# Products with v moved between the score units of an attention and feed-forward kernel

## The chip, the core and the metric

The kernel runs on one core of a Trainium2 chip. The metric is the device time of one execution in microseconds (us), the median of several runs. The engines are TensorE (PE in the profile, its weight loads PEld), VectorE (DVE), ScalarE (ACT), GpSimd (POOL) and SyncE (SP), which here issues nearly all DMAs.

## The reference

Attention with a decay from forget gates, for 4 batches of 8 heads with 576 queries and keys of 64 numbers, and then two feed-forward layers on the 2304 tokens of width 512, with 2048 hidden units:

```
scores = scale * q @ k.T
cum = cumsum(log(clip(f, 1e-4, 1)))
decay = cum[:, None] - cum[None, :]
attn = softmax(where(causal, -1e9, scores + decay))
x = attn @ v                       # heads laid side by side
h = x @ w_in;  x = (h - tanh(h)) @ w_out
h = x @ w_in2; out = (h * sigmoid(h)) @ w_out2
```

## The kernel before

The attention works on 16 pairs of heads, one after the other in a software pipeline. A pair is cut into nine score tiles, which form four **score units**: u = 0 has the first and second 128 queries of both heads (four tiles, with 128 and 256 keys), u = 1 the third 128 queries of both heads (384 keys), u = 2 the fourth (512 keys), u = 3 the last 64 queries of both heads together (576 keys, one tile, `pt`). Scores are computed with numbers split in a high and a low part (`kqs`), plus a product with the decay rows (`de`).

Each tile then goes through the engines. VectorE adds the mask and finds the row's minimum of the negated scores (`least`, tile `p` or `pt`, L462). ScalarE takes the exponent and the row sum (`expo`, L470). VectorE gathers three tiles' sums and takes reciprocals (`guard` L477, `normalise` L481). GpSimd scales three tiles (L484), in groups of tiles 0 to 2, 3 to 5 and 6 to 8 of a pair. TensorE transposes the scaled tiles in 128x128 blocks into PSUM tiles `t` (`transposes`, L495; 25 blocks a pair), VectorE and ScalarE copy them to `ptf` (`evac`, L535), TensorE multiplies `ptf` with `vraw` (`values`, L546), and ScalarE copies the result to `x` (`collect`, L554). Queries and keys of the next pair are split meanwhile: a cast of the keys on GpSimd (L383), a cast of the queries on VectorE (`split(p, 1)`, L385), and four subtractions on GpSimd (L391).

The order of everything is written by hand. The main loop runs over tile numbers n, nine to a pair, and every step is put at a number with `later` or `at`; each engine works through its own queue in that order. For pair p, with n0 = 9p, `steps_` gives the numbers of the transposes of the four units and of the values: n0 + 13, 15, 17, 18 and 26. Scores of a pair stand at n0 - 1, n0, n0 + 4 and n0 + 6. So while one pair is scored, the pair before it is transposed, and the values belong to the pair two before. `ends_` holds other numbers for the last two pairs. Score tiles have two PSUM buffers, transposed tiles (and a small output tile) three. In `transposes`, the fifth block of unit 3 takes a quarter of a PSUM tile, and the rest of that tile (`spare`) is used by unit 0 of the next pair.

The weights of the feed-forward part come as 64 bit numbers and are decoded in 14 steps a chunk (`wstages`): `scale` and `split` on ScalarE, `shift`, `exponent` and `low` on VectorE, `rest` and `join` (a subtraction and an addition, L176 and L180) on the engine `eng`. Chunks 0 and 1 are decoded during the attention, step by step at numbers spread evenly. The last part of the attention already has the first matmuls of the feed-forward part between its steps. The feed-forward part behind it isn't touched.

Of the kernel before, what the change touches and what calls it, by code (L numbers as in the profile page):

```python
# [7 lines left out]
F32 = mybir.dt.float32  # L8
# [6 lines left out]
P = 128  # L15
# [17 lines left out]
NEARLY, MID, LATE = 2, 3, 6  # L33
# [6 lines left out]
def forgetting_attention_two_ffn(  # L40
# [12 lines left out]
    nc = tc.nc  # L53
# [9 lines left out]
    def rd(ap):  # L63
        return ap.bitcast(F32)
# [21 lines left out]
    def setup_ident(const):  # L86
        ident = const.tile([P, P], F32, name="ident")
        nc.gpsimd.memset(ident, 0.0)
        nc.gpsimd.affine_select(
            out=ident, in_=ident, pattern=[[-1, P]], compare_op=ALU.not_equal,  # L90
            fill=1.0, base=0, channel_multiplier=1,
        )
        return ident
# [49 lines left out]
    def wstages(k):  # L143

        l, c = chunks[k]
        slot = k % NSLOT
        tag = {m: f"{l}_{c}_{m}" for m in range(2)}
        a, b, w = {}, {}, {}
        eng = nc.gpsimd if k < NEARLY + MID else nc.vector

        def scale(m):
            high = rd(raws[k, m][:, :, 1])
            nc.scalar.activation(high, high, AF.Prelu, scale=2.0 ** -112, alpha=-(2.0 ** 32))

        def shift(m):
            a[m] = wtmp.tile([P, DM], U32, tag="wa", name=f"wa{tag[m]}")
            nc.vector.tensor_scalar(a[m], raws[k, m][:, :, 1], 3, None, ALU.logical_shift_left)

        def split(m):
            hi, lo = w[m] = [  # L160
                wpool[slot].tile([P, DM], F32R, tag=f"w{s}{slot}_{m}", name=f"w{s}{tag[m]}") for s in "hl"
            ]
            nc.scalar.copy(hi, rd(a[m]))

        def exponent(m):
            b[m] = wtmp.tile([P, DM], F32, tag="wb", name=f"wb{tag[m]}")
            nc.vector.tensor_scalar(b[m].bitcast(U32), a[m], 0xFF800000, None, ALU.bitwise_and)

        def low(m):
            nc.vector.scalar_tensor_tensor(  # L170
                b[m], raws.pop((k, m))[:, :, 0], 2.0 ** -52, b[m], ALU.mult, ALU.mult
            )

        def rest(m):
            hi, lo = w[m]
            eng.tensor_tensor(lo, rd(a[m]), rd(hi), ALU.subtract)  # L176

        def join(m):
            hi, lo = w[m]
            eng.tensor_tensor(lo, rd(lo), b[m], ALU.add)  # L180
            wtiles[l, c, m] = (hi, lo)

        return [(fn, m) for fn in (scale, shift, split, exponent, low, rest, join) for m in range(2)]

    NSTAGE = 14
    stages = {}

    def wdecode(k, left=0):


        if k not in stages:
            stages[k] = wstages(k)
        while len(stages[k]) > left:
            fn, m = stages[k].pop(0)
            fn(m)
            if not stages[k] and k > 1:
                wload(k + 2)
# [7 lines left out]
    for l in range(2):  # L205
        c0 = 0
# [120 lines left out]
    def attention():  # L327
        with ExitStack() as actx:
# [4 lines left out]
            def pool(stack, name, bufs=1, **kw):  # L333
                return stack.enter_context(tc.tile_pool(name=name, bufs=bufs, side="right", **kw))
# [7 lines left out]
            ps_t = pool(actx, "ps_t", 3, space=PSUM)  # L342
# [4 lines left out]
            NP = B * NPAIR  # L347
# [5 lines left out]
            pt4 = [sp.tile([P, 640], F32, name=f"pt4_{i}", bufs=1) for i in range(2)]  # L353

            out_t = ps_r.tile([P, 512], F32, name="out_t")
            out_0, spare = {}, {}

            ptfs = [ptp.tile([P, 2, NPT], F32, name=f"ptf{i}") for i in range(2)]

# [58 lines left out]
            units = (((0, 0), (1, 0), (0, 1), (1, 1)), ((0, 2), (1, 2)), ((0, 3), (1, 3)), ((2, 4),))  # L418
            order = [t for unit in units for t in unit]
            NTILE = len(order)  # L420
            tiles = [(p, h, i) for p in range(NP) for h, i in order]
            N = len(tiles)
            sps, ptile, rowsum, tps = {}, {}, {}, {}
# [62 lines left out]
            def transposes(p, u):  # L486

                ptf = ptfs[p % 2]
                rest = spare.pop("t", None) if u == 0 else spare.clear()
                tp = [ps_t.tile([P, 4, P], F32, tag="t", name=f"t{p}_{u}_{j}") for j in range(1 if rest else 2)]  # L490
                if rest:
                    tp.append(rest[:, 1:])

                def turn(j, k, pt, c):
                    nc.tensor.transpose(tp[j][:, k], pt[:, c * P:c * P + P], ident)  # L495

                def place(j, c0, nc_, i):
                    n = 2 * nc_
                    q = P * i + 448 * c0
                    dst = ptf[:, :, q:q + 448 * nc_] if nc_ > 1 else ptf[:, :, q:q + P]  # L500
                    src = tp[j][:, 0:n]
                    if nc_ > 1:
                        dst = dst.rearrange("p h (c w) -> p h c w", w=448)[:, :, :, 0:P]
                        src = src.rearrange("p (h c) w -> p h c w", h=2)
                    return src, dst

                if u == 3:
                    ptile.pop((p, 2, 4))
                    pt = pt4[p % 2]
                    spare["t"] = tp[1]  # L510
                    for c in range(5):
                        turn(c // 4, c % 4, pt, c)
                    dst = ptf[:, :, 512:512 + 4 * 448].rearrange("p h (c w) -> p c h w", w=448)[:, :, :, 0:64]
                    o = 448 * 4 + 512
                    tps[p, u] = [
                        (tp[0].rearrange("p c (h w) -> p c h w", h=2), dst),
                        (tp[1][:, 0].rearrange("p (h w) -> p h w", h=2), ptf[:, :, o:o + 64]),
                    ]
                    return
                pts = {t: ptile.pop((p,) + t)[0] for t in units[u]}  # L520
                i = u + 1
                if u == 0:
                    for h in range(2):
                        turn(1, h, pts[h, 0], 0)
                for j in range(2 if u else 1):
                    for h in range(2):
                        for k in range(min(2, i + 1 - 2 * j)):
                            turn(j, min(2, i + 1 - 2 * j) * h + k, pts[h, i], 2 * j + k)
                tps[p, u] = [place(j, 2 * j, min(2, i + 1 - 2 * j), i) for j in range(2 if u else 1)]
                if u == 0:  # L530
                    tps[p, u].append(place(1, 0, 1, 0))

            def evac(p, u):
                for j, (src, dst) in enumerate(tps.pop((p, u))):
                    (nc.vector.tensor_copy if j == (u > 0) else nc.scalar.copy)(dst, src)  # L535

            def values(p, part):

# [56 lines left out]
            ident = setup_ident(const)  # L595
# [4 lines left out]
            def later(n, fn, *a):  # L600
                due.setdefault(max(n, 0), []).append((fn, a))
# [6 lines left out]
            for p in range(1, NP):  # L608
                n0 = NTILE * (p - 1)
                if p > 1:  # L610
                    if p > 2:
                        later(n0 - 9, load_kq, p)
                    later(n0 - 1, place_dec, p)
                    later(n0 - 1, place_dec_last, p)
                    later(n0 + (NTILE if p > 2 else 2 - NTILE), load_v, p)
                for j, k in enumerate((0, 0, 1, 2, 3, 4)):
                    later(n0 + k, split, p, j)
                later(n0 + 5, place_last, p)

            steps_ = (13, 15, 17, 18, 26)  # L620
            ends_ = {NP - 2: (13, 15, 17, 18, 20), NP - 1: (11, 12, 13, 14, 16)}
            for p in range(NP):
                n0 = NTILE * p
                for u, k in enumerate((-1, 0, 4, 6)):
                    if p + u:
                        later(n0 + k, scores, p, u)
                k = ends_.get(p, steps_)
                for u in range(4):
                    later(n0 + k[u], transposes, p, u)
                    later(n0 + k[u] + 1, evac, p, u)  # L630
                later(n0 + k[4], values, p, [(0, 0), (64, 0), (64, 1), (64, 2), (64, 3), (64, 4)])
                later(n0 + k[4] + 1, collect, p, 0, 64)
                later(n0 + k[4] + 1, collect, p, 64, S)
# [16 lines left out]
            def at(n, *item):  # L650
                ahead.setdefault(n, []).append(item)
# [3 lines left out]
                            (138, 3, 0), (140, 3, 1)):  # L655
                at(n - N, wload, k, (m,))
            for k in range(2 * NSTAGE):
                at((40, 87)[k // NSTAGE] + 46 * (k % NSTAGE) // NSTAGE - N,
                   wdecode, k // NSTAGE, NSTAGE - 1 - k % NSTAGE)
            for k in range(NKT):  # L660
                at(2 * k - 11, xsplit, 0, [k])
            for i in range(3):
# [80 lines left out]
```

## Time and profile before

| | before |
|---|---|
| median of 3 runs | 983.91 us (983.66 to 984.03) |
| profiled execution | 984.0 us, span 982.1 us |
| TensorE busy | 964.6 us, 98% |
| VectorE busy | 555.8 us, 57% |
| ScalarE busy | 454.8 us, 46% |
| GpSimd busy | 183.6 us, 19%, all of it in the first 208 us |
| granted TensorE clock | 1.000 |

Shares are over the whole span, of which the attention takes about the first 190 us. What a change in that part is worth has to be read there: from the windows and from the timeline of one pair. A timeline row gives the start, the time from the first start to the last end of the instructions it merges, the engine, the line, output <- inputs, the form, the count, and in brackets idle time ahead with what ended it.

### The profile page before, as it was taken

To read this page: it belongs to the slowest core of one execution; us is meant where nothing else is said; L and a number is where in the kernel's file an instruction comes from. 1 tells how busy PE (TensorE), PEld (TensorE's weight loads), DVE (VectorE), ACT (ScalarE), POOL (GpSimd) and SP (SyncE) were. 2 spreads that over 40 slices of the span, in tenths; PEclk is the share of its full clock that TensorE was granted. 3 is DMA by queue.
4 is the path that set the end of the run, shared out by engine and by line. 5 is a ranking of instruction groups with operands and counts; after the bars stand their busy time and mean duration, and the time that the engine had idled before them with its cause. 6 is when DMAs were issued, how large, how long until landed. Compare 5 with 4: busy or idle time off the path is not lost.

```text
span 982.1 us, 13857 instructions
## 1 busy us (share of the span) xinstructions
PE 964.6 (98%) x5208; PEld 791.5 (81%) x5208; DVE 555.8 (57%) x1221; ACT 454.8 (46%) x979; POOL 183.6 (19%) x266
## 2 busy tenths in 40 slices
PE   8999999999999999999999999999999999999998
PEld 6766666778988889888889888888888888888887
DVE  7667676686865456664668653354444544633323
ACT  6777777744543424343434443343444433433222
POOL 8979989740000000000000000000000000000000
PEclk9999999999999999999999999999999999999999
DMA  4433222421211011100112110111111000001111
GB/s 154 147 120 136 87 92 83 149 100 43 86 44 43 1 43 65 65 21 23 43 43 87 43 43 1 44 43 43 43 43 43 36 24 29 1 1 43 44 43 65
DMA packets 21699, 56.67 MB, mean 58 GB/s; under 512 B 6848, under 2 KB 6848, under 8 KB 21600
## 3 DMA queue, kind: packets, MB, share of 16 engines
q1 hardware_dynamic: 21624, 55.77, 16.1%
q8 instruction: 41, 0.67, 0.3%
q14 instruction: 26, 0.21, 0.1%
q10 hardware_dynamic: 8, 0.02, 0.0%
HBM read 49.35 MB, written 5.31 MB: 56 GB/s over the span
## 4 chain that ended last, share of the span: by engine, by line
PE 94%; DVE 3%; POOL 1%; issue 1%; DMA 0%; ACT 0%; SPq 0%; POOLq 0%; DVEq 0%
PE a L314 40%; PE h L255 39%; PE s L449 4%; PE out_t L546 4%; PE t L495 3%; PE s L441 2%; DVE p L462 1%; PE out_t L574 1%; POOL wl L180 1%; POOL wl L176 0%; DVE ptf L535 0%; PE out L546 0%; DMA kqraw<-kq 0%; DVE kqs L385 0%; POOL gl L277 0%
## 5 line engine op out<-in xcount | busy, mean ns | idle before, releaser
L255 PE MATMUL h<-xh,wl 128*128 128x512 f32 (+1 forms) x640 | 235.7, 368 | 2.2 <-POOL wl L180 2.2
L255 PE MATMUL h<-xh,wh 128*128 128x512 f32 (+1 forms) x640 | 236.0, 369 | 0.0
L255 PE MATMUL h<-xl,wh 128*128 128x512 f32 (+1 forms) x640 | 235.6, 368 | 0.0
L277 DVE TENSOR_TENSOR gl<-g,gh 128x512 fp32r<-128x512 f32 (+1 forms) x158 | 101.4, 642 | 99.9 <-ACT gh L273 98.0
L255 PEld LDWEIGHTS h<-xh,wl 128*128 128x128 f32 x640 | 120.6, 188 | 23.1 <-POOL wl L180 3.0
L255 PEld LDWEIGHTS h<-xh,wh 128*128 128x128 f32 x640 | 120.7, 189 | 20.6
L255 PEld LDWEIGHTS h<-xl,wh 128*128 128x128 f32 x640 | 120.6, 188 | 20.4
L273 ACT CAST gh<-g 128x512 fp32r<-128x512 f32 (+1 forms) x160 | 92.6, 579 | 95.8 <-DVE g L270 93.3
L314 PE MATMUL a<-gl,wh 128*128 128x512 f32 (+1 forms) x320 | 117.8, 368 | 0.0
L314 PE MATMUL a<-gh,wh 128*128 128x512 f32 (+1 forms) x320 | 117.7, 368 | 0.0
L314 PE MATMUL a<-gh,wl 128*128 128x512 f32 (+1 forms) x320 | 117.7, 368 | 0.0
L314 PE MATMUL a<-wh,gh 128*128 128x512 f32 x288 | 112.2, 390 | 0.0
L314 PE MATMUL a<-wl,gh 128*128 128x512 f32 x288 | 112.2, 390 | 0.0
L314 PE MATMUL a<-wh,gl 128*128 128x512 f32 x288 | 112.0, 389 | 0.0
L272 ACT ACTIVATE g<-h 128x512 f32<-128x512 f32 (+1 forms) x80 | 44.3, 554 | 113.6 <-PE h L255 96.3
L243 DVE TENSOR_TENSOR xl<-y,xh 128x512 fp32r<-128x512 f32 (+1 forms) x60 | 37.4, 638 | 96.6 <-ACT xh L241 96.6
L462 DVE CUSTOM_DVE_ANT_0 p<-s,mask 128x128 f32<-128x128 f32 (+3 forms) x128 | 59.9, 478 | 43.8 <-PE s L449 37.0
L241 ACT CAST xh<-y 128x512 fp32r<-128x512 f32 (+1 forms) x60 | 34.2, 580 | 104.8 <-PE h L255 103.1
L470 ACT ACTIVATE p<-p,mn 128x128 f32<-128x128 f32 (+3 forms) x128 | 71.1, 558 | 8.5 <-DVE mn L462 6.0
L484 POOL TENSOR_SCALAR p<-p,sm 128x128 f32<-128x128 f32 (+3 forms) x128 | 67.7, 548 | 18.3 <-DVE sm L481 18.3
L243 DVE TENSOR_TENSOR xl<-x,xh 128x512 fp32r<-128x512 f32 (+1 forms) x56 | 34.2, 632 | 61.6 <-ACT xh L241 61.6
L314 PEld LDWEIGHTS a<-gl,wh 128*128 128x128 f32 x320 | 60.3, 189 | 10.1
(92 smaller groups left out, 1388.9 us busy)
## 6 DMA issues: line engine op xcount, KB each, us to landing
raw<-w_in SPq DMA_DIRECT2D x32, 512.0 KB
raw<-w_out SPq DMA_DIRECT2D x32, 512.0 KB
kqraw<-kq SPq DMA_DIRECT2D x16, 608.0 KB
vraw<-v SPq DMA_DIRECT2D x16, 320.0 KB
out<-ob SPq DMA_DIRECT2D x18, 256.0 KB
lq<-kqs SPq DMA_DIRECT2D x32, 32.0 KB
dec<-x SPq DMA_DIRECT2D x1, 576.0 KB
de<-dec SPq DMA_DIRECT2D x28, 17.0 KB
```

The lines of the kernel that those rows point to most:

```text
L241: nc.scalar.copy(hi[:, :n], src[:, k, t0:t0 + n])
L243: eng.tensor_tensor(lo[:, :n], src[:, k, t0:t0 + n], rd(hi[:, :n]), ALU.subtract)
L255: nc.tensor.matmul(hp[:, :n], w[:, k * P:k * P + P], m[:, :n], start=(k == 0 and r == 0), stop=(k == NKT - 1 and r == 2),)
L272: nc.scalar.activation(g[:, :n], hp[:, :n], AF.Silu)
L273: nc.scalar.copy(gh[:, :n], g[:, :n])
L277: eng.tensor_tensor(gl[:, :n], g[:, :n], rd(gh[:, :n]), ALU.subtract)
L314: nc.tensor.matmul(dst, w, m, start=(first and r == 0), stop=(last and r == 2))
L449: nc.tensor.matmul(s[:, h, c:c + n], a[half(h), q], b[half(h), 0:n], start=r == 0, stop=r == 3,)
L462: nc.vector.tensor_tensor_reduce(out=pt.rearrange("p (g c) -> p g c", g=2) if i == 4 else pt, in0=src, in1=m, op0=ALU.add, op1=ALU.min, sc ...
L470: nc.scalar.activation(pt, pt, AF.Exp, bias=mn, scale=-1.0, accum_out=sums[:, n // 3 % 5, n % 3, 0:1],)
L484: nc.gpsimd.tensor_scalar(pt, pt, sm[:, j:j + 1], 1.0, ALU.mult, ALU.mult)
L546: nc.tensor.matmul(dst, vraw[p][:, h, D * c:D * c + D], ptfs[p % 2][:, h, 448 * c + a:448 * c + q1], start=c == 0, stop=c == last,)
```

## The change

It does four things. The values of a pair move from n0 + 26 to n0 + 22, that is, from behind the last transposes to between the second and the third score unit of the pair two behind, after unit 0's transposes. The transposes of unit 3 move from n0 + 18 to n0 + 15, into the call for unit 1 (three blocks of 128, 384 columns), except for the last pair: its fifth block goes into the half empty second PSUM tile of unit 1, its other four into a third tile. The cast of the queries moves from n0 to n0 - 1 of the pair before (n0 of `split`). And chunks 0 and 1 are decoded at other numbers, three steps to a pair from n = 37 to 118 (before: 40 to 82 and 87 to 129), their `rest` and `join` on VectorE in place of GpSimd.

```diff
-        eng = nc.gpsimd if k < NEARLY + MID else nc.vector
+        eng = nc.gpsimd if NEARLY <= k < NEARLY + MID else nc.vector
...
-                rest = spare.pop("t", None) if u == 0 else spare.clear()
-                tp = [ps_t.tile([P, 4, P], F32, tag="t", name=f"t{p}_{u}_{j}") for j in range(1 if rest else 2)]
-                if rest:
-                    tp.append(rest[:, 1:])
...
+                both = u == 1 and p < NP - 1
...
+                if u == 0:
+                    square(1, 0, 2, tile(0), 0, "V")
+                    square(0, 0, 1, tile(1), 0, "A")
+                elif u < 3:
+                    square(u + 1, 0, 2, tile(0), 0, "A")
+                    t = tile(1)
+                    square(u + 1, 2, u, t, 0, "V")
+                    if both:
+                        last_fifth(t, 2, "V")
+                        last_four(tile(2), "A")
+                else:
+                    last_four(tile(0), "A")
+                    last_fifth(tile(1), 0, "V")
...
-                for j, k in enumerate((0, 0, 1, 2, 3, 4)):
+                for j, k in enumerate((0, -1, 1, 2, 3, 4)):
...
-            steps_ = (13, 15, 17, 18, 26)
-            ends_ = {NP - 2: (13, 15, 17, 18, 20), NP - 1: (11, 12, 13, 14, 16)}
+            steps_ = (13, 15, 17, None, 22)
+            ends_ = {NP - 2: (13, 15, 17, None, 20), NP - 1: (11, 12, 13, 14, 16)}
...
-                for u in range(4):
+                for u in range(4 if k[3] else 3):
...
-                at((40, 87)[k // NSTAGE] + 46 * (k % NSTAGE) // NSTAGE - N,
-                   wdecode, k // NSTAGE, NSTAGE - 1 - k % NSTAGE)
+                at(NTILE * (4 + k // 3) + (1, 3, 5)[k % 3] - N, wdecode, k // NSTAGE, NSTAGE - 1 - k % NSTAGE)
```

`square`, `last_four` and `last_fifth` transpose the blocks of a unit and note the copy for `evac`; "A" is ScalarE and "V" VectorE. Copies stay on the engines they had, in size and number.

TensorE, one pair in the middle of the attention. In the names, `s_0` to `s_3` are the score units, `t_u_j` the transposed tiles of unit u, `out_` and `out_t` the products with v. Before:

```order
L449 MATMUL s_1_636<-kqs_498 128x384 x6
L449 MATMUL s_1_636<-de_103 128x384 x2
L495 MATMUL t_3_0_646<-ident,pt_1_107 128x128 x4
L495 MATMUL t_3_1_647<-ident,pt_1_107 128x128
L495 MATMUL t_3_1_647<-ident,p_0_446 128x128 x2
L495 MATMUL t_0_0_689<-ident,p_0_446 128x128 x4
L449 MATMUL s_2_696<-kqs_498 128x512 x6
```

After, at the same place:

```order
L449 MATMUL s_1_648<-kqs_484 128x384 x6
L449 MATMUL s_1_648<-de_103 128x384 x2
L496 MATMUL t_0_0_688<-ident,p_0_454 128x128 x4
L496 MATMUL t_0_1_693<-ident,p_0_454 128x128 x2
L552 MATMUL out_1_696<-ptf_110,vraw_194 64x64 x2
L552 MATMUL out_t<-ptf_110,vraw_194 64x512 x2
L552 MATMUL out_t<-ptf_110,vraw_194 64x448 x2
L552 MATMUL out_t<-ptf_110,vraw_194 64x320 x2
L552 MATMUL out_t<-ptf_110,vraw_194 64x192 x2
L552 MATMUL out_t<-ptf_110,vraw_194 64x64 x2
L449 MATMUL s_2_709<-kqs_484 128x512 x6
```

The transposes of unit 3 are gone from behind the second score unit, and the products with v stand in front of the third.

VectorE, from the reciprocal behind unit 3's minimum to the second minimum of the next pair (L385 is the cast of the queries). Before:

```order
L481 RECIPROCAL sm_624<-sm_624 128x3
L535 COPY ptf_110<-t_2_1_583 128x2x2x128
L462 ISA p_0_606,mn_0_0_658<-s_0_605,mask 128x128
L462 ISA mn_0_0_658 128x1
L385 TENSOR_REDUCE kqs_662<-kqraw_501 128x640
L535 COPY ptf_110<-t_3_1_647 128x2x64
L462 ISA p_0_606,mn_1_0_672<-s_0_605,mask 128x128
```

After:

```order
L481 RECIPROCAL sm_634<-sm_634 128x3
L385 TENSOR_REDUCE kqs_646<-kqraw_502 128x640
L541 COPY ptf_110<-t_2_1_610 128x2x2x128
L462 ISA p_0_616,mn_0_0_661<-s_0_615,mask 128x128
L462 ISA mn_0_0_661 128x1
L462 ISA p_0_616,mn_1_0_671<-s_0_615,mask 128x128
```

The cast stands ahead of the copy of unit 2 instead of behind the first minimum, and the copy of unit 3's fifth block is gone from here (it follows a copy of unit 1).

## Rows read from the trace of the kernel before

**Rows 1.** Windows: us, then busy time per engine, clock, DMA.

```profile
core 0: us, PE busy (x) PEld busy (x) DVE busy (x) ACT busy (x) POOL busy (x), PEclk, DMA share, GB/s
33.88:44.58 10.70, 10.14 (x90) 7.42 (x89) 7.05 (x30) 7.66 (x25) 9.42 (x16) 1.00 0.54 198
```

**Rows 2.** Waits from 18 to 175 us: waiting <- waited for: us, times, longest.

```profile
DVE p L462 <- PE s L449: 34.5, 13, 3.4
...
PEld s L449 <- DVE mn L462: 6.3, 16, 0.9
PE t L495 <- DVE ptf L535: 6.2, 13, 0.5
```

**Rows 3.** Timeline of TensorE's weight loads, one pair.

```profile
33.87 0.20 PEld L546 LDWEIGHTS out<-ptf,vraw 128*64 128x64 f32 x4 [0.17 <-issue]
...
36.73 0.41 PEld L449 LDWEIGHTS s<-kqs 64*128 64x128 f32 x6
...
38.55 0.53 PEld L495 LDWEIGHTS t<-ident,pt 128*128 128x128 f32 x5 [0.25 <-issue]
39.76 0.64 PEld L495 LDWEIGHTS t<-ident,p 128*128 128x128 f32 x6 [0.68 <-POOL kqs L391]
40.72 0.53 PEld L449 LDWEIGHTS s<-kqs 64*128 64x128 f32 x6 [0.33 <-DVE mn L462]
...
41.85 0.64 PEld L495 LDWEIGHTS t<-ident,p 128*128 128x128 f32 x6 [0.36 <-issue]
42.45 0.43 PEld L441 LDWEIGHTS s<-kqs,lq 128*128 128x128 f32 x3
...
43.48 0.93 PEld L495 LDWEIGHTS t<-ident,p 128*128 128x128 f32 x8
44.58 0.20 PEld L546 LDWEIGHTS out<-ptf,vraw 128*64 128x64 f32 x4 [0.17 <-issue]
```

**Rows 4.** Timeline of TensorE's matmuls: third score units of pairs 1, 2 and 15.

```profile
21.71 0.96 PE L449 MATMUL s<-kqs 64*128 64x512 f32 x6 [0.64 <-DVE mn L462]
...
30.02 0.96 PE L449 MATMUL s<-kqs 64*128 64x512 f32 x6
...
170.97 0.96 PE L449 MATMUL s<-kqs 64*128 64x512 f32 x6
```

**Rows 5.** Timeline of GpSimd: early, one pair, and a place with weight decoding.

```profile
23.11 0.76 POOL L484 TENSOR_SCALAR pt<-pt,sm 128x576 f32<-128x576 f32 x1
...
35.03 2.76 POOL L484 TENSOR_SCALAR p<-p,sm 128x128 f32<-128x128 f32 x6
37.75 0.69 POOL L383 TENSOR_SCALAR kqs<-kqraw 128x576 fp32r<-128x576 f32 x1
38.52 0.80 POOL L391 TENSOR_TENSOR kqs<-kqraw,kqs 128x288 fp32r<-128x288 f32 x1
40.52 1.36 POOL L484 TENSOR_SCALAR p<-p,sm 128x512 f32<-128x512 f32 x2 [1.20 <-DVE sm L481]
41.86 0.75 POOL L484 TENSOR_SCALAR pt<-pt,sm 128x576 f32<-128x576 f32 x1
42.57 2.47 POOL L391 TENSOR_TENSOR kqs<-kqraw,kqs 128x288 fp32r<-128x288 f32 x3
...
143.27 3.17 POOL L484 TENSOR_SCALAR p<-p,sm 128x128 f32<-128x128 f32 x6
```

**Rows 6.** Timeline of VectorE: minimum of unit 3, and the reciprocal behind it.

```profile
43.93 0.76 DVE L462 CUSTOM_DVE_ANT_0 pt<-s,mask 128x576 f32<-128x576 f32 x1
...
44.61 0.17 DVE L481 RECIPROCAL sm<-sm 128x3 f32<-128x3 f32 x1
```

**Rows 7.** Weight decoding: lines (busy, mean ns), and durations of L170 (least, middle, longest).

```profile
L176 POOL TENSOR_TENSOR wl<-wa,wh 128x512 fp32r<-128x512 f32 x10 | 13.5, 1363 | 0.0
L176 DVE TENSOR_TENSOR wl<-wa,wh 128x512 fp32r<-128x512 f32 x6 | 3.9, 684 | 0.0
...
L170 DVE SCALAR_TENSOR_TENSOR wb<-raw,wb x4: 685/964/1294, 84.1 to 144.0; 128x512 f32<-128x512 uint32 x4
```

**Rows 8.** Timeline of TensorE where the feed-forward part begins.

```profile
200.73 0.50 PE L255 MATMUL h<-xh,wl 128*128 128x512 f32 x1 [1.66 <-POOL wl L180]
```

More of the change, by code (lines that the diff above doesn't have):

```diff
@@ L355, in attention @@
             out_t = ps_r.tile([P, 512], F32, name="out_t")
-            out_0, spare = {}, {}
+            out_0 = {}
             ptfs = [ptp.tile([P, 2, NPT], F32, name=f"ptf{i}") for i in range(2)]
@@ L488, in transposes @@
                 ptf = ptfs[p % 2]
-                rest = spare.pop("t", None) if u == 0 else spare.clear()
-                tp = [ps_t.tile([P, 4, P], F32, tag="t", name=f"t{p}_{u}_{j}") for j in range(1 if rest else 2)]
-                if rest:
-                    tp.append(rest[:, 1:])
[L494 to L505, printed above, removed]
@@ L507, in transposes @@
-                if u == 3:
-                    ptile.pop((p, 2, 4))
[L509 to L519, printed above, removed]
@@ L520, in transposes @@
-                pts = {t: ptile.pop((p,) + t)[0] for t in units[u]}
-                i = u + 1
-                if u == 0:
[L523 to L529, printed above, removed]
@@ L530, in transposes, with tile, turn, move @@
-                if u == 0:
-                    tps[p, u].append(place(1, 0, 1, 0))
+                tps[p, u] = moves = []
+                both = u == 1 and p < NP - 1
+                def tile(j):
+                    return ps_t.tile([P, 4, P], F32, tag="t", name=f"t{p}_{u}_{j}")
+                def turn(t, k, pt, c):
+                    nc.tensor.transpose(t[:, k], pt[:, c * P:c * P + P], ident)
+                def move(eng, src, dst):
+                    moves.append((nc.scalar.copy if eng == "A" else nc.vector.tensor_copy, dst, src))
@@ new lines, in square @@
+                def square(i, c, n, t, k, eng):
+                    for h in range(2):
+                        for j in range(n):
+                            turn(t, k + n * h + j, pts[h, i], c + j)
+                    src, q = t[:, k:k + 2 * n], P * i + 448 * c
+                    if n == 1:
+                        return move(eng, src, ptf[:, :, q:q + P])
+                    dst = ptf[:, :, q:q + 448 * n].rearrange("p h (c w) -> p h c w", w=448)[:, :, :, 0:P]
+                    move(eng, src.rearrange("p (h c) w -> p h c w", h=2), dst)
@@ new lines, in last_four, with last_fifth @@
+                def last_four(t, eng):
+                    for c in range(4):
+                        turn(t, c, pt4[p % 2], c)
+                    dst = ptf[:, :, 512:512 + 4 * 448].rearrange("p h (c w) -> p c h w", w=448)[:, :, :, 0:64]
+                    move(eng, t.rearrange("p c (h w) -> p c h w", h=2), dst)
+                def last_fifth(t, k, eng):
+                    turn(t, k, pt4[p % 2], 4)
+                    o = 448 * 4 + 512
+                    move(eng, t[:, k].rearrange("p (h w) -> p h w", h=2), ptf[:, :, o:o + 64])
@@ new lines, in transposes @@
+                pts = {t: ptile.pop((p,) + t)[0] for t in units[u]}
+                if both:
+                    ptile.pop((p, 2, 4))
+                if u == 0:
+                    square(1, 0, 2, tile(0), 0, "V")
[4 more added lines that the diff above has]
+                    square(u + 1, 2, u, t, 0, "V")
+                    if both:
+                        last_fifth(t, 2, "V")
[3 more added lines that the diff above has]
+                    last_fifth(tile(1), 0, "V")
@@ L533, in evac @@
             def evac(p, u):
-                for j, (src, dst) in enumerate(tps.pop((p, u))):
-                    (nc.vector.tensor_copy if j == (u > 0) else nc.scalar.copy)(dst, src)
+                for fn, dst, src in tps.pop((p, u)):
+                    fn(dst, src)
             def values(p, part):
```

## Prediction, made before the changed kernel had run

> **What bounds the kernel now.** I read the windows by engine first, then the waits, then the timeline of one pair of heads on TensorE and on GpSimd. The feed-forward part behind the attention is not touched, so only the attention part can give anything. One pair period there is 10.70 us, and TensorE is busy for 10.14 of them; GpSimd 9.42, ScalarE 7.66, VectorE 7.05 [rows 1]. The busy share flatters TensorE, as ends of matmuls are modelled; the weight loads show the real gaps [rows 3]. The waits to look at are few: the first transposes of the next pair wait for a VectorE copy 13 times, 6.2 us in all; the loads of the third score unit wait for VectorE's minima 16 times, 6.3 us; and VectorE itself idles 34.5 us for scores [rows 2]. That last one is the root: while TensorE multiplies with v (2.86 us, from the load at 33.87 to that at 36.73), no score is made, VectorE runs dry, and afterwards everything that hangs on its minima is late.
>
> Call the score units s0 to s3, their transposes t0 to t3, the products with v V. From the starts of the loads [rows 3] one period reads: V 2.86; s0 and s1 36.73 to 38.55, 1.82; t3 to 39.76, 1.21, of which the loads take 0.53 and 0.68 is wait; t0 to 40.72, 0.96, with 0.33 of wait at its end; s2 to 41.85, 1.13; t1 to 42.45, 0.60; s3 to 43.48, 1.03; t2 to 44.58, 1.10 with a gap of 0.17. Sum 10.71.
>
> **The change part by part.** (1) New order on TensorE: s0, s1, t0, V, s2, t1 with t3, s3, t2. No matmul is added or dropped. With the same pieces: s0 and s1 1.82; t0 0.64 and the gap 0.17 that stood between t2 and V, 0.81; V 2.86; s2 1.13; t1 with t3 0.60 + 0.53 = 1.13; s3 1.03; t2 1.10, whose gap I keep, for s0 in V's place. Sum 9.88, that is 0.83 less a pair: the waits of 0.68 and 0.33 go, 0.17 comes. The first wait was that t0 wrote into the rest of t3's PSUM tile while VectorE copied the fifth block out of it; now t0 has a tile of its own and t3's fifth block goes into t1's. Eight such tiles a pair turn over three buffers before and after.
>
> What is late next? GpSimd's normalised tiles: t0 stood behind s1 and t3, now it stands right behind s1. GpSimd runs in a ring: six tiles 2.76, the query and key parts 0.69 and 0.80, two tiles 1.36, the last queries 0.75, three parts 2.47, sum 8.83 [rows 5]; against 9.88 it has 1.05 to spare. The tile that t0 needs is the fourth of the six, and waits for the reciprocal that VectorE makes behind the minimum of s3. After s3's last stretch (to 43.48) that minimum starts at 43.93 and the reciprocal ends at 44.78 [rows 6]; with one tile of 2.76/6 = 0.46 the tile is there 1.76 after 43.48, while TensorE needs t2 and s0, s1, 1.10 + 1.82 = 2.92, to come to t0. Spare 1.16. So I cost it at nothing; if GpSimd has no room, it is the first rival's price. V needs t2's copies, which have s0, s1 and t0 (2.63) as cover; s2 needs the minima of s0, with V as cover, more than two microseconds beyond the 0.33 that it waits now.
>
> (2) The cast of the queries goes one step earlier in VectorE's queue, ahead of t2's copy. It lies in the spare time just named. Its DMA was issued a period earlier, except for the fourth pair, near 28 us; that is in the head, below. No DMA of SyncE changes its place.
>
> (3) Weight decoding of chunks 0 and 1: eight subtractions and additions leave GpSimd, 8 x 1.36 = 10.9 us, and come to VectorE, 8 x 0.68 = 5.5 us when nothing disturbs them [rows 7]. The 28 steps of the two chunks now stand three to a pair, behind the minima of s0, of s0 and of s1, where VectorE idled. In the heaviest pairs VectorE then has 7.05 + 2.3 (one product at 0.96 and two at 0.68 [rows 7]) = 9.4 of 9.88. Queued behind them are the minima and the copy of t0; TensorE asks for those only after V. Bounds: nothing at all, up to 0.2 us for each of the ten pairs with steps. I take 0.07 a pair as a mean over all periods (estimate, nearer to nothing because of V's 2.86).
>
> (4) Disturbances. From s2 at 30.02 to s2 at 170.97 lie 13 periods [rows 4], 140.95 us, 10.84 each. That is 0.13 a period over the 10.71, 1.7 us in all, from decode steps that today sit between minima. With V behind t0 they have cover, so I let them go; kept, they cost 1.7.
>
> (5) Head. The first s2 behind s0, s1 waits 0.64 for a minimum [rows 4], which goes as the cast is early. But t3 of pair 0 now stands in front of s3 and needs the last queries normalised, ready at 23.11 + 0.76 = 23.87 [rows 5], about 1 us after t1 is done; VectorE's cast for the fourth pair also waits for its load there. Against that, t3 (1.21 with its wait) is out of the way later. Between -0.6 and +1.2; I take a gain of 0.5.
>
> (6) End. Products of pair 13 and t3 of pair 14 leave the stretch behind the last scores and stand before. It is the same work. The 1.66 us that TensorE waits for a decoded weight at 200.73 [rows 8] hang on the last products of all, whose place among the matmuls behind them is kept: no gain.
>
> Sum: 13 x (10.84 - 9.95) = 11.6, with 0.5 of the head 12.1. The profiled execution took 984.0 us (span 982.1, 1.9 around it), the median of the runs is 983.9; 984.0 - 12.1 = 971.9, said as 972.
>
> **The rivals.** First, GpSimd becomes the bound. For it: six tiles that took 2.76 took 3.17 at 143.27 [rows 5], while VectorE decoded. If its whole ring is stretched so, 8.83 x 3.17/2.76 = 10.14, and the period is that: 13 x (10.14 - 9.95) = 2.5 more, 974.4. Narrower and dearer: the decode steps with two SBUF operands disturb GpSimd. On VectorE the product of this kind took 0.69 to 1.29 us, 0.96 in the middle, while GpSimd worked [rows 7]: one of the two was held up. There are 12 such steps in 28, in six pairs 1, 3, 2, 2, 3 and 1. If GpSimd stands still for 0.68 in each, and 1.05 a pair is spare, two pairs lose 0.99 and two 0.31: 2.6 us, 974.6; at 1.29 it is 9.2 us, 981.2.
>
> The Trainium skill speaks against this part of the change: "SBUF — State Buffer", section "SBUF: two separate sides", says that a VectorE operation with two SBUF inputs and a GpSimd operation that reads SBUF exclude each other for a whole instruction. By that rule moving the subtractions to VectorE gives back much of what GpSimd is spared; the spread from 0.69 to 1.29 agrees with it, and the time would be that of the rival just worked out.
>
> Second, the wait only changes its name. If GpSimd kept its place in time, s1 would end at 33.87 + 1.82 = 35.69, while the fourth of the six tiles, four sixths of 2.76 from 35.03 [rows 5], is done at 36.87: 1.18 us of wait a pair, against 0.83 of gain and 0.13 of disturbances. That is 0.22 x 13 = 2.9 slower, with the head 986; at a wait of 0.96 the two cancel, 984. Against it: GpSimd starts its ring late only because it waits 1.20 for a reciprocal [rows 5] that stands behind s0, and s0 behind V; that comes forward too.
>
> Third, slower: VectorE, now without its pauses, stretches every GpSimd operation. The point is a ring of 10.84, 23% over 8.83; 15% is what 143.27 shows. At 30% the ring is 11.48 and the time 13 x 0.64 = 8.3 above, 992. Only a stretch twice as large as seen gives this.
>
> That the order is not what is said is ruled out by the rows of the program.
>
> **How the numbers follow.** Forecast, TensorE bound with 9.8 to 10.05 a period: 0.62, 972, its own range 969 to 974. First rival, both forms: 0.22, 974 to 981. Second: 0.10, half of it about 984 and half slower. Third: 0.06. A measurement of this kernel tells about 0.2%, 2 us, from no change. Faster: 0.62 + 0.21 = 0.83, as the dearest end of the first rival comes to within 3 us of no change; same 0.05 + 0.01, and 0.01 of the third in a mild form, 0.07; slower 0.05 + 0.05 = 0.10. The range goes from 968.5 (period 9.7, head at its best) to 978.5, where the forecast and most of the first rival lie.
>
> **What would show it.** In the profile after: a pair period of about 9.9 on TensorE, no wait of t0 for a VectorE copy, VectorE's idle time for s0 gone from 3.4 a pair to small pieces, GpSimd idle for about 1 us a pair for the reciprocal behind s3. A wait of TensorE for normalised tiles at t0 or t3 in most pairs would show the first or second rival; in four pairs with decode steps only, the rule on the two SBUF inputs. I am wrong if the transposes of t0 wait for GpSimd all along, or if a period stays above 10.2.

## The result and the profile after

The changed kernel took 970.75 us (median of 4 runs, 970.68 to 970.82) where the kernel before took 983.78 beside it (4 runs, 983.47 to 984.03): a ratio of 0.9868, 95% interval 0.9851 to 0.9885. It is 13.0 us faster; the prediction said 12.1 (972.0, range 968.5 to 978.5). The profiled execution took 970.75 with a span of 968.6, against a span of 982.1 before.

First the page of the changed kernel: its span.

```profile
span 968.6 us, 13856 instructions
```

The gain must come from the attention part, so the next view is the period of one pair. In the timeline of TensorE's matmuls after the change (start, duration, instruction, idle time before it and its releaser) the third score unit of pairs 1, 2 and 15 answers to [rows 4], and the transposes of the last queries in the head stand between:

```profile
20.97 0.98 PE L449 MATMUL s<-kqs 64*128 64x512 f32 x6
...
23.89 0.77 PE L496 MATMUL t<-ident,pt 128*128 128x128 f32 x5 [0.91 <-POOL pt L484]
...
32.01 0.98 PE L449 MATMUL s<-kqs 64*128 64x512 f32 x6
...
160.59 0.96 PE L449 MATMUL s<-kqs 64*128 64x512 f32 x6
```

From 32.01 to 160.59 lie 13 periods, 128.58 us, 9.89 each; before it was 140.95, 10.84 each [rows 4]. That is 12.37 of the 13.5 us by which the span is shorter. The head gives 0.87: before, s2 of pair 2 stood at 30.02 with its V of 2.86 still to come, 32.88 in all, now it stands at 32.01 with that V behind it. Behind the last s2, again without the V of 2.86 that still had to come there, the span before had 982.1 - 170.97 - 2.86 = 808.27 left; now 968.6 - 160.59 = 808.01 are left, another 0.26. These three make the 13.5.

One period piece by piece, in the timeline of TensorE's weight loads after the change; it answers to [rows 3]:

```profile
61.72 0.53 PEld L449 LDWEIGHTS s<-kqs 64*128 64x128 f32 x6
...
62.85 0.64 PEld L496 LDWEIGHTS t<-ident,p 128*128 128x128 f32 x6 [0.37 <-issue]
63.45 0.58 PEld L496 LDWEIGHTS t<-ident,pt 128*128 128x128 f32 x5
64.00 0.43 PEld L441 LDWEIGHTS s<-kqs,lq 128*128 128x128 f32 x3
...
65.04 0.93 PEld L496 LDWEIGHTS t<-ident,p 128*128 128x128 f32 x8
66.13 0.41 PEld L449 LDWEIGHTS s<-kqs 64*128 64x128 f32 x6 [0.17 <-issue]
...
67.95 0.64 PEld L496 LDWEIGHTS t<-ident,p 128*128 128x128 f32 x6 [0.25 <-issue]
68.75 0.20 PEld L552 LDWEIGHTS out<-ptf,vraw 128*64 128x64 f32 x4 [0.17 <-issue]
...
71.61 0.30 PEld L449 LDWEIGHTS s<-kqs 64*128 64x128 f32 x4
```

Read by starts: s2 1.13, t1 0.60, t3 0.55, s3 1.04, t2 1.09, s0 and s1 1.82, t0 0.80, V 2.86, sum 9.89. No releaser in it is another engine. The page's waits between 18 and 165 us (engine, line and what it waited for: us in total, times, longest) answer to [rows 2]:

```profile
DVE p L462 <- PE s L449: 18.8, 13, 2.4
...
PEld t L496 <- POOL pt L484: 3.0, 6, 1.1
...
PEld s L449 <- DVE mn L462: 0.3, 2, 0.2
```

TensorE's 13 waits for a VectorE copy, 6.2 us, have no row any more; its loads wait for minima 0.3 us in place of 6.3; VectorE's idle time for scores is 18.8 in place of 34.5. It hasn't gone to small pieces, as the prediction's signs had it: VectorE is no longer idle for s0's scores, but while TensorE multiplies with v it now idles for those of s2 (1.69 at 53.18, up to 2.4), which TensorE hardly feels. Of the 3.0 us that loads wait for normalised last queries, 1.1 stand in the head; the other five, of 0.36, are as long as the gap at 62.85, which has no other engine behind it, and add nothing. Where GpSimd stands shows in the windows of two periods (columns as in [rows 1]: us, then busy time and instructions of TensorE, its loads, VectorE, ScalarE and GpSimd, granted clock, DMA share, GB/s), one without decode products and one with them:

```profile
51.84:61.72 9.88, 9.88 (x93) 7.45 (x89) 7.43 (x30) 8.60 (x28) 8.88 (x15) 1.00 0.34 109
81.50:91.38 9.88, 9.88 (x93) 7.45 (x89) 9.53 (x33) 7.78 (x25) 9.80 (x15) 1.00 0.26 76
```

TensorE sets the period in both. But the same 15 GpSimd instructions take 8.88 in the first and 9.80 in the second: the spare time of 1.0 is used up there to 0.08.

### The profile page after: what moved, and what is told of

Its sections match the earlier page's. It is cut to its first block, busy times and chain, and to the rows that moved or that the text cites. A ratio compares the mean times of both kernels' runs of the same rounds, so it can differ in the third digit from the quotient of the medians.

```text
span 968.6 us, 13856 instructions
## 1 busy us (share of the span) xinstructions
PE 959.9 (99%) x5208; PEld 791.7 (82%) x5208; DVE 564.3 (58%) x1229; ACT 456.6 (47%) x979; POOL 177.6 (18%) x258
## 4 chain that ended last, share of the span: by engine, by line
PE 97%; POOL 1%; DVE 1%; issue 0%; DMA 0%; ACT 0%; POOLq 0%; SPq 0%
PE a L314 40%; PE h L255 40%; PE s L449 5%; PE t L496 5%; PE out_t L552 4%; PE s L441 2%; PE out_t L580 1%; POOL wl L176 0%; PE out L552 0%; POOL wl L180 0%; DMA raw<-w_in 0%; DVE wa L157 0%; DVE p L462 0%; ACT ptf L541 0%; POOL de L572 0%
```

## The experiments

All times are medians, beside the kernel before run on the same chip (983.54 to 983.88). The period is from one V to the next.

| kernel | us | ratio (95%) | period, undisturbed | periods with decode steps |
|---|---|---|---|---|
| changed | 970.75 | 0.9868 (0.9851 to 0.9885) | 9.89 | 9.88 to 9.89 |
| t3_back | 979.77 | 0.9964 (0.9950 to 0.9978) | 10.56 | 10.56 |
| v_back | 983.43 | 0.9997 (0.9987 to 1.0006) | 10.14 | 10.42 to 11.29 |
| v_back_old | 985.62 | 1.0016 (1.0006 to 1.0026) | 10.13 | up to 14.04 |
| order_only | 977.75 | 0.9938 (0.9923 to 0.9953) | 9.89 | up to 12.38 |
| old_weights | 978.02 | 0.9938 (0.9923 to 0.9952) | 9.89 | up to 12.37 |
| pool_weights | 975.09 | 0.9913 (0.9898 to 0.9927) | 9.89 | up to 11.34 |
| cast_back | 971.09 | 0.9870 (0.9856 to 0.9885) | 9.89 | 9.88 to 9.89 |
| no_order | 988.21 | 1.0047 (1.0032 to 1.0062) | 10.69 | up to 11.80 |
| pool_1 | 975.29 | 0.9916 (0.9901 to 0.9931) | 9.89 | up to 11.02 |
| pool_3 | 998.80 | 1.0152 (1.0135 to 1.0169) | none | 11.57 to 13.67 |
| dve_2 | 973.56 | 0.9899 (0.9884 to 0.9914) | 9.89 to 9.92 | up to 11.00 |
| late_dve | 967.76 | 0.9837 (0.9821 to 0.9853) | 9.89 | 9.88 to 9.89 |

### t3_back: is it the shared PSUM tile that t0 waited for?

The kernel before, with V at its new place and the cast and the weights as changed; t3 keeps its old place and t0 its rest of t3's tile.

```diff
-            steps_ = (13, 15, 17, 18, 26)
+            steps_ = (13, 15, 17, 18, 22)
```

> The kernel before with the products with v between the second and third score unit, the early cast and the new weight decoding, but with unit 3's transposes in their old place and old PSUM tiles (the rest of a tile used by unit 0). If the shared PSUM tile causes the wait of t0 for VectorE's copy, that wait of 0.5 to 0.7 a pair stays and the period is about 10.5: 979. If the wait came from VectorE running late for want of scores, the products' new place removes it too: 971 to 973.

979.77, so t3's move with its own tile for t0 is worth 9.0 us, 13 times 0.69. The timelines of VectorE and of TensorE in this kernel show the copy of t3's fifth block, and the wait as it was before:

```profile
49.02 0.29 DVE L535 COPY ptf<-t 128x128 f32<-128x128 f32 x1 [0.91 <-PE t L495]
```

```profile
48.21 0.77 PE L495 MATMUL t<-ident,pt 128*128 128x128 f32 x5
49.45 0.85 PE L495 MATMUL t<-ident,p 128*128 128x128 f32 x6 [0.47 <-DVE ptf L535]
```

The copy ends at 49.31 and t0 starts at 49.45. The wait stands there in all 13 periods, and each is 10.56 long, 0.67 above 9.89. The step of the prediction that took 0.68 for it holds. (The later place of t3 and the tile of its own for t0 come together; no run has one without the other.) That these periods are all alike, although VectorE decodes in ten of them, shows more: with V between the first two score units and s2, the decode steps are free.

### v_back and v_back_old: what V's place is worth

The changed kernel with V behind t2 again, first with the new decoding, then also with the old engine and numbers of the decoding (as in old_weights below).

```diff
-            steps_ = (13, 15, 17, None, 22)
+            steps_ = (13, 15, 17, None, 26)
```

> The changed kernel with the products with v put back behind the last transposes (n0 + 26); unit 3's transposes, the cast and the weights stay as changed. If the products are what gives VectorE its head start, the minima of unit 0 come late again: s2 then starts 0.9 us behind s1's end instead of the 0.64 that t0 takes, and t3 in front of s3 meets GpSimd's last queries about 0.5 us too early: a period of 10.0 to 10.4 instead of 9.89, time 972.5 to 977.5, with waits of TensorE for minima or for normalised tiles in most pairs. If the place of the products is nearly all of the gain: 981 or more. If only the move of unit 3's transposes and the cast counts: 971 to 972.

> The new place of unit 3's transposes and the early cast, the products with v at n0 + 26 as before, and all weight decoding as before on GpSimd. With the new decoding this order had periods of 10.4 us in the pairs without decoding steps and 10.7 to 11.3 in those with. If the decoding between unit 0's minima on VectorE is what took the rest, this kernel has about 10.4 in most pairs against 10.84 before: 978 to 980.5. If the products' place is all that counts, however the weights are decoded: 983 to 984.

Both missed. v_back took 983.43: taking back V's place alone loses the whole gain. Yet its first, undisturbed period is 10.14, only 0.25 above 9.89, 3.3 us over 13. Two waits make it, in the timeline of TensorE's loads in v_back: s2's for a minimum, after which s2 starts 0.11 later behind t0 than V does in the changed kernel, and t3's for the last queries, after which it starts 0.81 behind t1 in place of 0.60:

```profile
40.71 0.53 PEld L449 LDWEIGHTS s<-kqs 64*128 64x128 f32 x6 [0.26 <-DVE mn L462]
...
42.64 0.53 PEld L496 LDWEIGHTS t<-ident,pt 128*128 128x128 f32 x5 [0.17 <-POOL pt L484]
```

The periods with decode steps make the rest: the 13 periods from V at 35.14 to V at 174.33 take 139.19 us, 7.4 more than 13 of 10.14. With 1.7 of head and end this is the 12.4 by which the span (981.0) is longer. Waits between 18 and 165 us in v_back:

```profile
DVE p L462 <- PE s L449: 29.1, 12, 2.9
...
PEld s L449 <- DVE mn L462: 7.2, 15, 0.9
...
PE t L496 <- POOL pt L484: 4.4, 7, 1.4
...
```

How this comes about is seen at one place, in the timeline of VectorE and of TensorE in v_back. A decode product stands ahead of the minima that s2 waits for:

```profile
92.73 0.29 DVE L462 CUSTOM_DVE_ANT_0 p<-s,mask 128x128 f32<-128x128 f32 x1 [2.46 <-PE s L449]
...
93.16 0.69 DVE L180 TENSOR_TENSOR wl<-wl,wb 128x512 fp32r<-128x512 f32 x1
...
94.26 0.40 DVE L462 CUSTOM_DVE_ANT_0 p<-s,mask 128x256 f32<-128x256 f32 x1
```

```profile
94.72 0.95 PE L449 MATMUL s<-kqs 64*128 64x512 f32 x6 [0.63 <-DVE mn L462]
...
97.19 0.77 PE L496 MATMUL t<-ident,pt 128*128 128x128 f32 x5 [0.49 <-POOL pt L484]
```

VectorE is dry for 2.46 us while TensorE multiplies with v, and then has the decode step in the way; s2 waits 0.63 and, further on, t3 0.49 for the normalised last queries.

v_back_old shows that the old decoding doesn't help there: 985.62. Its undisturbed periods are 10.13 as well (the 10.4 of the expectation was misread), but two are 14.04 and 12.35. The longer one in the timelines of GpSimd and of TensorE:

```profile
104.22 1.28 POOL L180 TENSOR_TENSOR wl<-wl,wb 128x512 fp32r<-128x512 f32 x1
...
106.80 0.74 POOL L484 TENSOR_SCALAR pt<-pt,sm 128x576 f32<-128x576 f32 x1
```

```profile
107.60 1.07 PE L496 MATMUL t<-ident,pt 128*128 128x128 f32 x5 [2.25 <-POOL pt L484]
```

The last queries are normalised at 107.54, behind a decode step of 1.28, and t3, which now stands in front of s3, waits 2.25 for them. So with V in its old place neither form of the decoding keeps any of the gain. V's new place without t3's move and without the new decoding was not run.

### order_only, old_weights, pool_weights, cast_back, no_order: the parts apart

The edits put back single lines of the change. old_weights puts back the engine and the numbers of the decoding, pool_weights the engine alone, cast_back the cast, order_only all three; no_order is the kernel before with the early cast and the new decoding.

```diff
-        eng = nc.gpsimd if NEARLY <= k < NEARLY + MID else nc.vector
+        eng = nc.gpsimd if k < NEARLY + MID else nc.vector
...
-                for j, k in enumerate((0, -1, 1, 2, 3, 4)):
+                for j, k in enumerate((0, 0, 1, 2, 3, 4)):
...
-                at(NTILE * (4 + k // 3) + (1, 3, 5)[k % 3] - N, wdecode, k // NSTAGE, NSTAGE - 1 - k % NSTAGE)
+                at((40, 87)[k // NSTAGE] + 46 * (k % NSTAGE) // NSTAGE - N,
+                   wdecode, k // NSTAGE, NSTAGE - 1 - k % NSTAGE)
```

> The changed kernel with only TensorE's new order: weights decoded on GpSimd at the old numbers, the cast of the queries at its old place. By GpSimd's ring of 8.83 us with about 1 us to spare against 9.89, the four pairs that decode on GpSimd (2.7 us each) lose about 1.6 each and the cast costs up to 0.6 at the head: 976 to 978. If the order on TensorE is all that counts: 971. If GpSimd is the bound throughout: above 980.

> The changed kernel with all of the weight decoding as before: on GpSimd and at the old numbers, only the order and the early cast are new. By the ring's spare 976 to 978, like the run with the order alone; if spreading matters more than the engine, this is worse than the run with GpSimd at the new numbers.

> The changed kernel with the subtractions and additions of chunks 0 and 1 back on GpSimd, at the new numbers. They stand in pairs of 2, 2, 3 and 1 steps of 1.36 us. Against about 1 us of spare in GpSimd's ring that is a loss of 1.7, 1.7, 3.0 and 0.3: 977. If GpSimd has more room than that or TensorE has tiles in stock: 971 to 973.

> The changed kernel with the cast of the queries back at its old place, between the first two minima of unit 0. By the sum it lies in spare time either way: 970.8 to 971.5, the most at the head (0.6). If VectorE's queue behind the cast holds up unit 0's minima and with them the normalised tiles: 0.5 a pair or more, 977.

> The kernel before with only the early cast and the new weight decoding, TensorE's order as before. By my sum the disturbances of 1.7 and 0.6 at the head go, 981.5; the cast out of the way of unit 0's minima may also take the 0.33 that s2 waits in each pair, down to 978. If these two parts are only there to make room for the new order: 983.8.

The new order without the new decoding keeps 5.9 us of the 13.0 (order_only 977.75, old_weights 978.02), about as expected. In old_weights the undisturbed periods are 9.88 to 9.92, and five others carry the loss: 11.48, 10.61, 10.68, 12.37 and 11.00, the last where 9.30 stands in the changed kernel. Together that is 7.3 us, what the two kernels differ by (978.02 - 970.75 = 7.27). Four of the five are GpSimd's: it is busy for all or nearly all of them. The last, 11.00, is not: TensorE's granted clock falls there, behind a wait of 1.25 that ends at 162.82, and the twenty matmuls of V at 163.57 take 4.46 in place of 2.76. In the window of that stretch, in old_weights:

```profile
163.40:168.00 4.60, 4.60 (x27) 1.99 (x26) 1.21 (x5) 1.73 (x7) 4.60 (x6) 0.63 1.03 393
```

That is 1.7 of the 7.3. In the profiled execution of order_only (976.55, clock 1.00) the same place has a period of 9.32, and the one execution of old_weights whose mean clock is 1.000 took 976.41, the others 977.99 to 978.15.

TensorE in old_weights, in the first of the five, where t0 waits for a normalised tile:

```profile
99.50 0.66 PE L496 MATMUL t<-ident,p 128*128 128x128 f32 x4 [1.26 <-POOL p L484]
```

pool_weights, with the new numbers but the products on GpSimd, was expected at 977 and took 975.09; its four long periods (10.56, 11.24, 11.34, 10.62) add 4.2. So the even spread of the steps alone, with the same engine, is worth 2.9 us against old_weights (1.7 of it the lower clock that old_weights has), and the move to VectorE the other 4.3. GpSimd in one of them, in pool_weights:

```profile
85.76 1.17 POOL L484 TENSOR_SCALAR p<-p,sm 128x128 f32<-128x128 f32 x3
86.90 1.28 POOL L176 TENSOR_TENSOR wl<-wa,wh 128x512 fp32r<-128x512 f32 x1
88.17 1.61 POOL L484 TENSOR_SCALAR p<-p,sm 128x256 f32<-128x256 f32 x3
```

A product of 1.28 stands in the middle of the six tiles, just ahead of the fourth, the one that t0 needs. So the move of the products to VectorE is not a side matter of the change: under the new order GpSimd has 1.0 a period to spare, and one product takes 1.28.

cast_back took 971.09, 0.34 more than the changed kernel, and no period changes. The first s2 waits 0.64 for its minimum again, but t3 behind it waits only 0.22 for the last queries in place of 0.91, so the one pays for the other. What cast_back loses in the head stands ahead of both: its s0 starts at 18.80, in the changed kernel at 18.34. order_only, with the cast at the old place too, has its s0 at 18.32 and comes to s2 of pair 2 at 32.02, the changed kernel at 32.01. TensorE in order_only:

```profile
21.66 0.96 PE L449 MATMUL s<-kqs 64*128 64x512 f32 x6 [0.64 <-DVE mn L462]
...
23.91 0.77 PE L496 MATMUL t<-ident,pt 128*128 128x128 f32 x5 [0.25 <-POOL pt L484]
...
32.02 0.97 PE L449 MATMUL s<-kqs 64*128 64x512 f32 x6
```

So no run shows a gain from the early cast. Why s0 comes 0.46 later in cast_back isn't shown.

no_order missed, on the other side: 988.21, 4.6 slower than before. Under the old order the decode steps that moved to VectorE stand between the minima with V already past, and the periods grow to 11.80. TensorE in no_order keeps t0's old wait of 0.47, and the matmuls of s2 wait 0.69 for a minimum; their loads wait 0.93 there, against 0.33 in [rows 3]:

```profile
97.02 0.96 PE L449 MATMUL s<-kqs 64*128 64x512 f32 x6 [0.69 <-DVE mn L462]
```

### pool_1, pool_3 and dve_2: how much room is left

The changed kernel with work added in 12 pairs. pool_1 and pool_3 repeat one subtraction of the last split on GpSimd (0.87 us each) once and three times; dve_2 puts two more casts behind the first minima on VectorE. Everything else is as changed.

```diff
+                if p > 3 and j == 5:
+                    for _ in range(N):
+                        eng.tensor_tensor(lo[:, c0:c1], raw[p][:, c0:c1], rd(hi[:, c0:c1]), ALU.subtract)
```

```diff
+                if p > 3 and j == 2:
+                    c = slice(S, RAW)
+                    for _ in range(2):
+                        nc.vector.tensor_reduce(hi[:, c], raw[p][:, c].rearrange("p (n o) -> p n o", o=1), axis=AX.X, op=ALU.max)
```

> The changed kernel with one more subtraction on GpSimd in each of 12 pairs (the last part of the next pair's queries is split a second time, the same numbers), about 0.86 us, in front of the normalising. If GpSimd has about 1 us to spare in its ring, as the sum had it, nothing in the pairs without decoding and a few tenths in those where GpSimd is slowed: 970.8 to 972.5. If GpSimd is on the edge already: 12 x 0.86 more, 981.

> As the run before with three such subtractions, 2.6 us in each of 12 pairs. With 1.05 to spare the ring becomes 8.83 + 2.6 = 11.4 against 9.89: 12 x 1.5 = 18 more, 989, TensorE waiting for normalised tiles in each pair. If GpSimd is not part of the ring that I named, 971 to 973; if it is already the bound, 12 x 2.6 = 31 more, 1002.

> The changed kernel with the cast of the queries done twice more on VectorE in each of 12 pairs, 2 x 0.75 to 0.8 us, behind the first minima of unit 0, while TensorE multiplies with v. If the products with v cover VectorE there, the pairs without decoding lose nothing and the heavy ones (7.05 + 2.3 + 1.6 = 10.95 against 9.89) up to 1.1 in four pairs: 971 to 975.5. If VectorE is on TensorE's path, 12 x 1.6 more: 990.

pool_1 missed: 975.29, 4.5 more than the changed kernel. Until 78.63 its periods hold at 9.89, so 0.87 does fit in the spare time of an undisturbed pair. In pairs with decode products it doesn't, because there GpSimd's own work is longer: the six tiles that take 2.77 at 55.47 take 3.75 at 86.74. One more long period (10.97, from 151.60) has no such product; there a subtraction of the feed-forward part's input, 1.28 on GpSimd at 160.19, stands between the tiles. GpSimd's timeline in pool_1, and the wait of t0 that follows the tiles:

```profile
86.74 3.75 POOL L487 TENSOR_SCALAR p<-p,sm 128x128 f32<-128x128 f32 x6
```

```profile
88.98 0.66 PE L499 MATMUL t<-ident,p 128*128 128x128 f32 x4 [0.57 <-POOL p L487]
```

pool_3 was expected at 989, from a GpSimd ring of 8.83 + 3 x 0.87 = 11.44, and took 998.8. No period there is under 11.44 once the added work is in full swing, so GpSimd is the bound, as expected. But the periods go up to 13.67. The window of the longest in pool_3:

```profile
73.33:87.00 13.67, 11.11 (x90) 7.66 (x89) 11.71 (x41) 9.15 (x28) 13.35 (x19) 0.96 0.44 158
```

GpSimd is busy for all but 0.32 us of it, and for all but 0.32 of each of the ten others between 49.75 and 185.17. The eleven add up to 135.4, 9.6 more than eleven of 11.44: the time above the expectation is GpSimd's own work, with the small gaps in it, being longer than the sum said. TensorE's granted clock falls in some of these periods (0.85 in that from 61.73 to 73.33, one of the shortest with 11.60), but doesn't set their length.

dve_2 took 973.56, 2.8 more, inside what was expected. Its undisturbed periods stay at 9.89 to 9.92; only those with decode steps grow (10.08 to 11.00). VectorE has room, in most pairs, for two more casts.

### late_dve: a faster version

Where the feed-forward part begins, TensorE still waits twice for a weight decoded on GpSimd in the changed kernel, at 187.28 and 193.54; the first answers to [rows 8]. The timelines of TensorE and, ahead of the wait, of GpSimd after the change:

```profile
187.28 0.50 PE L255 MATMUL h<-xh,wl 128*128 128x512 f32 x1 [1.68 <-POOL wl L180]
...
193.54 0.50 PE L255 MATMUL h<-xh,wl 128*128 128x512 f32 x1 [0.52 <-POOL wl L180]
```

```profile
181.85 1.30 POOL L277 TENSOR_TENSOR gl<-g,gh 128x512 fp32r<-128x512 f32 x1 [3.51 <-ACT gh L273]
...
185.78 1.45 POOL L180 TENSOR_TENSOR wl<-wl,wb 128x512 fp32r<-128x512 f32 x1
```

GpSimd waits 3.51 for another operand and only then decodes. The edit takes chunks 3 and 4 off it too:

```diff
-        eng = nc.gpsimd if NEARLY <= k < NEARLY + MID else nc.vector
+        eng = nc.gpsimd if k == NEARLY else nc.vector
```

> The changed kernel with the subtractions and additions of chunks 3 and 4 on VectorE too; only chunk 2 stays on GpSimd. In the profile after, TensorE waits 1.68 us at 187.28 and 0.52 at 193.54 for these on GpSimd, which stand behind a subtraction that itself waits 3.51 for ScalarE. On VectorE they can start when their inputs are there: 968.6. If VectorE, which decodes at the same time, becomes as late as GpSimd was: 970.8.

967.76 (967.71 to 967.81), 3.0 below the changed kernel and the fastest of all. Both waits are gone. The windows from 182 to 200 us, of the changed kernel and then of late_dve:

```profile
182.00:200.00 18.00, 15.80 (x68) 12.43 (x68) 15.06 (x16) 7.96 (x15) 12.75 (x9) 1.00 0.30 104
```

```profile
182.00:200.00 18.00, 18.00 (x81) 14.93 (x80) 16.27 (x29) 9.73 (x18) 1.56 (x1) 1.00 0.28 108
```

TensorE issues 81 matmuls in this stretch in place of 68, 13 more. They follow each other at 18.00/81 = 0.22, which makes 2.9 us, so the gain lies here, though the waits that the profile names sum to only 2.2 (busy time counts modelled ends). VectorE has 1.73 of the 18 us left.

## Why the prediction was right, and where its terms were off

**TensorE's order (1).** Right. The sum of pieces was 9.88 and the period is 9.89; t1 with t3 is 1.15 (predicted 1.13), t0 0.80 (0.81), t2 1.09 (1.10). t3_back shows that t0's wait came from the shared PSUM tile, and prices it at 0.67 a period. So the root that the prediction names, VectorE running dry for scores, is not the root of this larger part: in t3_back V has moved and the wait stays. V's place is worth another 0.25 in a period without decode steps: the waits of s2 and of t3.

**What is late next.** Nothing, in the end, but by less than the prediction said. GpSimd's ring is 8.88 in an undisturbed period (8.83 predicted), and it waits for the reciprocal, as foretold; but the spare time shrinks with each decode product. GpSimd's timeline after the change, ahead of its last three tiles, in two pairs following each other:

```profile
66.50 1.60 POOL L484 TENSOR_SCALAR p<-p,sm 128x256 f32<-128x256 f32 x3 [0.96 <-DVE sm L481]
...
76.39 1.61 POOL L484 TENSOR_SCALAR p<-p,sm 128x256 f32<-128x256 f32 x3 [0.35 <-DVE sm L481]
...
85.31 2.74 POOL L484 TENSOR_SCALAR p<-p,sm 128x128 f32<-128x128 f32 x6
```

It idles 0.96 at 66.50, 0.35 at 76.39, and one pair later runs through all six tiles without a pause. So the GpSimd bound was near: pool_1 fell into it with 0.87 us more.

**The first rival's mechanism is real, and its price was half.** The rival had GpSimd stand still for 0.68 in each product with two SBUF operands on VectorE. VectorE and GpSimd do hold each other up: products that take 0.68 undisturbed took up to 1.23 (at 79.28) in the changed kernel. In VectorE's timeline:

```profile
89.33 1.22 DVE L180 TENSOR_TENSOR wl<-wl,wb 128x512 fp32r<-128x512 f32 x1
```

In the window from 81.50 three such products (at 82.13, 87.74 and 89.33) stand against 0.92 us more of GpSimd, 0.31 each in place of 0.68. Three of them were to lose 0.99 a period; they fit with 0.08 to spare. The rule of the Trainium skill ("SBUF — State Buffer", section "SBUF: two separate sides"), that the two exclude each other for a whole instruction, agrees with the lengthened instructions on both engines. By the same section of the Trainium skill the one that starts first holds the shared ports and the other waits, so either engine can lose; that agrees too, for here VectorE bears about half (0.18 + 0.16 + 0.54 = 0.88 on the three products, which last 0.86, 0.84 and 1.22).

**The second and third rival** didn't come. Behind the head no wait of TensorE for a normalised tile is longer than the gap that stands there without one (0.37 and 0.25 in the period shown), and GpSimd comes forward with the reciprocal.

**Early cast (2).** Costed at nothing in the period, and that is what cast_back shows. In the head it is worth nothing either, by order_only.

**Weights (3).** Mis-sized a little: 0.07 a period was taken as a mean over all 13, and the periods with and without decode steps differ by 0.01. The cover that the prediction named, V, is the reason. What it costs if the cover is gone was not priced, and the runs price it: 7.4 us in v_back, 4.6 in no_order against the kernel before. This is where my expectations of v_back, v_back_old and no_order went wrong: I summed parts that aren't additive. Decoding on VectorE without V as cover loses time, the new order with decoding on GpSimd keeps less than half of the gain, and only together do they make 13.0.

**Disturbances (4).** The 1.7 us went, as forecast: 13 x 9.89 = 128.57, with the 9.89 that the pieces of one period add up to, is what is measured over the 13 (128.58), with no remainder.

**Head and end (5, 6).** The head gave 0.87 where 0.5 was taken, inside its bounds of -0.6 to 1.2; the wait of t3 behind t1, put at about 1 us, is 0.91 at 23.89. That the term came so near is in part luck: the 0.64 that s2 no longer waits was counted as a gain, and by order_only t3's wait, 0.91 in place of 0.25, takes it back. What is left comes from the next pair, out of which t3 has gone. The end gave 0.26 where nothing was taken. These 0.37 and 0.26, and the 0.9 that (3) was too dear, less 0.13 for 13 periods of 9.89 in place of 9.88, make the 1.4 us between the 12.1 and the 13.5 of the two spans.

## What to carry to other kernels

A long block of matmuls that depends on nothing recent is the cover for whatever the other engines must do between two dependent steps, so put it where their queues are behind, and then move their side work under it. Here the order alone kept 5.9 of 13.0 us, and the side work alone lost 4.6. Price a cover by what happens without it, since parts that share one don't add up. When an engine has 1 us a period to spare, look at how long its instructions get beside a busy neighbour before spending it.

## What was not expected of the hardware

VectorE's products of 0.68 us took up to 1.23, and six tiles on GpSimd 3.75 in place of 2.77 (in pool_1), where the two engines ran such steps beside each other, though neither waited for the other by the profile.

TensorE's granted clock fell within the attention part when it had waited. In the windows of v_back_old around the wait of 2.25 us:

```profile
104.00:107.60 3.60, 1.36 (x12) 0.75 (x8) 1.59 (x7) 2.75 (x9) 3.60 (x6) 1.00 0.18 72
107.60:111.82 4.22, 4.22 (x21) 4.04 (x21) 2.38 (x9) 2.34 (x6) 3.58 (x7) 0.60 0.06 12
```

TensorE was busy for 1.36 of 3.60 us, and in the 4.22 behind it the mean granted clock was 0.60, so for most of that stretch the lower level of 1.2 GHz in place of 2.4. The period is 14.04 long, 3.91 over the undisturbed one, of which the named wait is 2.25. Most of the rest is the lower clock: from t3 to V TensorE takes 4.22 here, and 2.64 in v_back (42.64 to 45.28) at a clock of 1.00. In old_weights the same came behind a wait of 1.25, and cost 1.7, but not behind the one of 1.26 at 99.50, nor behind one of 2.15 at 163.17 in v_back_old (2.63 from t3 to V, clock 1.00). So a wait can be paid a second time, in matmuls that wait for nothing; which waits are, these runs don't tell. In the changed kernel and in late_dve the clock is 1.00 in every window shown, also behind the waits of 0.91, 1.68 and 0.52.
